# The second channel group's products of a gated dynamic convolution, from stacked 12-bit parts on the whole array to plain float32 on half of its rows

## The chip, the cores and the metric

One core of a Trainium2 chip runs the kernel: TensorE (PE in the profile, its weight loads PEld), VectorE (DVE), ScalarE (ACT), GpSimd (POOL) and SyncE (SP), which here only issues DMAs. The metric is the device time in microseconds from the first to the last instruction of the core. Three runs of the kernel before took 647.55, 649.92 and 651.01 us; the median is 649.92.

## The reference, cut to what matters

Eight sequences of 4224 rows with 192 channels (D), 8 heads of 24 channels. First a dynamic convolution whose weights are a softmax over 7 taps for each row and head, then a gated value path:

```
w   = softmax(weight_gen, axis=-1)                    # (B, S, 8, 7)
x1  = sum over k of w[.., k] * x[row - 6 + k]         # per head, 24 channels
gate = sigmoid(sum over k of conv_w[k] * x1[row - 4 + k])   # 5 taps per channel
val  = x1 @ w_val                                     # 192 x 192
out  = (gate * val) @ w_out                           # 192 x 192
```

All of it is float32 to the reader; weights of the value path come as float64 and are rounded.

## The kernel before, in words

**Tiling.** The rows are cut into blocks of 384 (BLK), and two blocks make a macro; there are 44 macros (NM). Channels live in partitions, in two groups. Group 0 ("A" tiles) is 128 channels of one block, so a macro has two such slices. Group 1 ("B" tiles) is the other 64 channels, those of the macro's first block in partitions 0 to 63 and those of its second block in 64 to 127. Tiles A, B and S (a staging tile for the channels of the last two heads) are allocated for a pair of macros, an even one and the odd one behind it, and rotate through two buffers: the tile of macros 6 and 7 takes the place of that of macros 2 and 3.

**Stages of a macro.** `bank` (L355) does the dynamic convolution as 16 small matmuls for each of four PSUM banks (tile pa, three buffers); `evac` (L393, L395, L399) copies them into A, B and S on ACT, and `moves` sends parts of S into A and B by DMA. `tap0` (ACT, L421, L424) and `tap` (DVE, L429) build the gate's argument in aA and aB, `sigm` (ACT, L433) the gate. `split_a` writes A as a high part of 12 bits (hi, ACT, L440) and the rest (lo, POOL, L441). `split_b` does the same for B through `stack`, which puts the high part of a block's 64 channels in its own half of the partitions and the low part in the other half (tile q, ACT L447, POOL L448), and `gsplit` does it for the gated values of group 1 (tile g, the same two lines).

**Products.** `val` (L462) makes block k's values for group 0 in five fp32r matmuls of 384 columns: two from q, three from hi and lo; for group 1 (k = 2) it uses plain float32 (L464 on the whole array, L466 on two halves of its columns, one per block). `gv` (DVE, L473) multiplies by the gate. `omm` (L489 to L491) makes two chunks of 128 output rows per call: for each one two fp32r matmuls from g (256 columns, against woh and wob) and one float32 matmul from aA (192 columns). There are three calls per macro, each with one PSUM tile po out of two buffers, and `oev` (ACT, L499) copies each into ot, which goes out by DMA.

**What sets the order.** The kernel schedules by hand: `at(t, f)` notes a piece of work with a time in macros, PLAN gives the offsets, and the pieces are emitted in order of time. Every engine then executes its own instructions strictly in the order emitted, and waits where a tile that it reads is not written yet, or where a buffer that it takes over still has a reader.

Of the kernel before, what the change touches and what calls it, by code (L numbers as in the profile page):

```python
# [16 lines left out]
# The order in which the parts of the macros' work are emitted: each at the macro's index plus a number from here.  # L17
# [7 lines left out]
    splitB=2.7981,  # L25
# [5 lines left out]
    gsplit=3.8257,  # L31
# [8 lines left out]
    spo=(2.2858, 3.439),  # L40
# [14 lines left out]
def tile_dynconv_gated_moe(  # L55
# [9 lines left out]
    nc = tc.nc  # L65
# [78 lines left out]
    def order_weights():  # L144
        """Rows of the weights in DRAM in the order of their channels in the partitions."""
# [16 lines left out]
    def convert_weights(raw, cs, v, w):  # L162
        """raw, float64 in pairs of words (low, high), rounded to float32 in columns cs of wf."""
# [19 lines left out]
    def split_weights():  # L183
        """The columns of w_val in the order of the channels in the partitions: towards the first group as sums
        of two parts of 12 bits each, towards the second as they are. The second group's rows of w_out as such
        sums too."""
        units = []

        def runs(dst, src, q0, q1):
            """Quadrants q0 .. q1 - 1 of the columns: (dst, src) for both runs of channels in them."""  # L190
            d = dst.rearrange("p (a c) -> p a c", c=Q)
            return ((d[:, :, 0:C], src[:, C * q0:C * q1].rearrange("p (a c) -> p a c", c=C)),
                    (d[:, :, C:Q], src[:, c6 + HC * q0:c6 + HC * q1].rearrange("p (a c) -> p a c", c=HC)))
# [7 lines left out]
        for g in (1, 0):  # L201
            for (h, v), (l, _) in zip(runs(wvh[:, g], wf[:, g, 0:D], 0, 4), runs(wvl[:, g], wf[:, g, 0:D], 0, 4)):
                units.append(lambda h=h, v=v: nc.scalar.copy(out=h, in_=v))
                units.append(lambda h=h, l=l, v=v: nc.gpsimd.tensor_tensor(
                    out=l, in0=v, in1=h.bitcast(FP32), op=ALU.subtract))
            if g == 1:
                for b in range(2):
                    hs = slice(HD * b, HD * b + HD)
                    units.append(lambda b=b, hs=hs: nc.scalar.copy(out=wvb[b][hs], in_=wvl[hs, 1].bitcast(FP32)))
        s = wf[:, 1, D:2 * D]  # L210
        out_units = [lambda: nc.scalar.copy(out=woh[:, 0:D], in_=s)]
        for b in range(2):
            hs = slice(HD * b, HD * b + HD)
            out_units.append(lambda b=b, hs=hs: nc.gpsimd.tensor_tensor(
                out=wob[b][hs, 0:D], in0=s[hs], in1=woh[hs, 0:D].bitcast(FP32), op=ALU.subtract))
        return units, out_units
# [150 lines left out]
    def pair(i, name, shape):  # L367
        """The tile of that name of macros i and i ^ 1."""
# [12 lines left out]
    def stir(n):  # L381
        """Work of no effect that keeps the clock of the tensor engine up while the first loads are on the way."""
# [18 lines left out]
    def moves(i, g):  # L401
        """Fill the holes of macros i - 1 and i, or of i alone where it is the only one left."""
# [40 lines left out]
    def stack(src, dst, eng):  # L443
        """dst[:, u]: the high part of block u's half of src in its own half, the low part in the other."""
        for u in range(2):
            own, oth = slice(HD * u, HD * u + HD), slice(HD - HD * u, P - HD * u)
            nc.scalar.copy(out=dst[own, u], in_=src[own])  # L447
            eng.tensor_tensor(out=dst[oth, u], in0=src[own], in1=dst[own, u].bitcast(FP32), op=ALU.subtract)  # L448

    def split_b(i):  # L450
        s = st[i]
        s["q"] = work.tile([P, 2, BLK], FP32R, name="q")
# [209 lines left out]
```

## Time and profile before

| What | Value |
|---|---|
| median of three runs | 649.92 us (647.55 to 651.01) |
| the profiled execution's own time, its span | 650.0 us |
| mean granted TensorE clock | 0.971 |
| PE busy | 582.7 us |
| DVE busy | 601.7 us |
| ACT busy | 438.0 us |
| POOL busy | 376.6 us |
| start of the fourth macro's L464, of the 41st's | 106.31 us, 604.28 us |

The profile is one execution. An engine's busy time is the union of its instructions; those of PE overlap, so the sum over its lines is more than its busy time. Each macro has one L464 on PE, so the starts of L464 cut the span into macros: in the text, a macro's period runs from one L464 to the next. Times in a row are microseconds from the start of the span.

### The profile page before, as it was taken

The page shows a single profiled execution, that of the slowest core. Times are in us where ns is not written, and L with a number is a line of the kernel's source. Part 1 is how long each engine was busy: PE and PEld are TensorE (multiplying, and loading weights), DVE is VectorE, ACT ScalarE, POOL GpSimd, SP SyncE. Part 2 cuts the span into 40 slices and gives each one's busy share as a digit, 9 for nine tenths or more (in the row PEclk, how much of TensorE's full clock was granted, in tenths as well). Part 3 has the DMA queues.
Part 4 walks back from the last instruction along what each step waited for, and adds up shares of the span by engine and source line. Part 5 has one row for each costly group of instructions (what it writes and reads, how often), then busy time and mean ns, then how long its engine had stood idle before and what let it go on. Part 6 is the DMA issues. An engine that isn't in the chain of part 4 may idle for free.

```text
span 650.0 us, 18233 instructions
## 1 busy us (share of the span) xinstructions
PE 582.7 (90%) x7422; PEld 459.1 (71%) x7422; DVE 601.7 (93%) x653; ACT 438.0 (67%) x789; POOL 376.6 (58%) x292
## 2 busy tenths in 40 slices
PE   1356699998998999997999979998998999999976
PEld 0345477876787778775778857787876887788766
DVE  7867999999999899998999989998999998898994
ACT  4436396687748687586776768757966676667763
POOL 9154744774755645572665727556656556455673
PEclk9986799999999999999999999999998999999998
DMA  6879967997896968987598876997878658754313
GB/s 191 225 244 176 315 154 167 282 247 155 176 291 197 203 145 206 295 227 154 125 275 214 224 158 129 247 248 188 197 196 288 156 135 196 168 123 114 86 44 110
DMA packets 126914, 124.65 MB, mean 192 GB/s; under 512 B 9390, under 2 KB 121354, under 8 KB 126062
## 3 DMA queue, kind: packets, MB, share of 16 engines
q1 hardware_dynamic: 122970, 101.25, 65.3%
q0 software_dynamic: 3840, 22.23, 9.2%
q8 instruction: 59, 0.97, 0.7%
q14 instruction: 25, 0.20, 0.1%
q10 hardware_dynamic: 20, 0.01, 0.0%
HBM read 67.12 MB, written 50.36 MB: 181 GB/s over the span
## 4 chain that ended last, share of the span: by engine, by line
PE 45%; DVE 22%; DMA 19%; issue 4%; SPq 4%; ACT 4%; POOL 1%; DVEq 0%; ACTq 0%; POOLq 0%
PE pa L355 21%; DVE aA L429 9%; PE po L491 7%; DVE aB L429 6%; PE pv L462 5%; DMA tb<-zd 4%; DMA A<-S 4%; PE po L489 4%; DMA wt<-in_weight_gen_dram 3%; DMA zd<-zt 3%; PE pv L464 3%; PE pv L466 3%; PE po L490 3%; DVE zt L280 2%; SPq L334 2%
## 5 line engine op out<-in xcount | busy, mean ns | idle before, releaser
L355 PE MATMUL pa<-tb,xt 106*32 106x96 f32 (+1 forms) x5632 | 267.9, 357 | 37.4 <-ACT wt L260 22.2
L355 PEld LDWEIGHTS pa<-tb,xt 106*32 106x32 f32 x5632 | 206.7, 129 | 100.3 <-issue 63.1
L429 DVE SCALAR_TENSOR_TENSOR aA<-A,wf,aA 128x768 f32<-128x768 f32 x176 | 226.2, 1286 | 2.5 <-ACT aA L421 2.5
L429 DVE SCALAR_TENSOR_TENSOR aB<-B,wf,aB 128x384 f32<-128x384 f32 x176 | 193.5, 1100 | 0.0
L448 POOL TENSOR_TENSOR q<-B,q 64x384 fp32r<-64x384 f32 x88 | 112.3, 1277 | 99.6 <-ACT q L447 66.1
L441 POOL TENSOR_TENSOR lo<-A,hi 128x768 fp32r<-128x768 f32 x44 | 93.8, 2132 | 101.9 <-issue 35.2
L448 POOL TENSOR_TENSOR g<-aB,g 64x384 fp32r<-64x384 f32 x88 | 126.6, 1439 | 12.9 <-ACT g L447 6.4
L491 PE MATMUL po<-wf,aA 128*128 128x192 f32 x528 | 131.1, 330 | 2.1 <-DVE aA L473 2.1
L489 PE MATMUL po<-woh,g 128*128 128x256 f32 x264 | 98.9, 374 | 17.6 <-ACT ot L499 12.9
L491 PEld LDWEIGHTS po<-wf,aA 128*128 128x128 f32 x528 | 81.8, 191 | 2.6 <-DVE aA L473 2.5
L499 ACT COPY ot<-po 128x384 f32<-128x384 f32 x132 | 62.7, 476 | 25.2 <-PE po L491 24.2
L489 PEld LDWEIGHTS po<-woh,g 128*128 128x128 f32 x264 | 50.4, 191 | 35.4 <-ACT ot L499 15.2
L490 PE MATMUL po<-wob,g 128*128 128x256 f32 x264 | 74.4, 282 | 0.0
L393 ACT COPY A<-pa 128x388 f32<-128x388 f32 x88 | 41.2, 481 | 46.3 <-PE pa L355 27.5
L399 ACT COPY S<-pa 64x388 f32<-64x388 f32 x88 | 42.2, 479 | 29.9 <-PE pa L355 29.3
L473 DVE TENSOR_TENSOR aA<-pv,aA 128x384 f32<-128x384 f32 x88 | 48.1, 547 | 7.3 <-ACT aA L433 6.3
L490 PEld LDWEIGHTS po<-wob,g 128*128 128x128 f32 x264 | 50.6, 192 | 0.0
L421 ACT ACTIVATE aA<-A,wf 128x768 f32<-128x768 f32 x44 | 41.4, 941 | 12.7 <-DMA A<-S 9.1
L447 ACT CAST g<-aB 64x384 fp32r<-64x384 f32 x88 | 45.0, 512 | 4.6 <-DVE aB L473 2.7
L395 ACT COPY B<-pa 128x388 f32<-128x388 f32 x44 | 21.3, 483 | 38.0 <-DVE aB L429 17.8
L433 ACT ACTIVATE aA<-aA 128x768 f32<-128x768 f32 x44 | 37.4, 851 | 13.6 <-DVE aA L429 13.4
L447 ACT CAST q<-B 64x384 fp32r<-64x384 f32 x88 | 44.5, 506 | 1.1
(74 smaller groups left out, 711.0 us busy)
## 6 DMA issues: line engine op xcount, KB each, us to landing
xt<-in_x_dram SPq DMA_DIRECT2D x35, 672.0 KB
out_dram<-ot SPq DMA_DIRECT2D x39, 576.0 KB
tb<-zd SPq DMA_DIRECT2D x240, 88.0 KB
zd<-zt POOLq DMA_DIRECT2D x21, 968.0 KB, 6.8
wt<-in_weight_gen_dram SPq DMA_DIRECT2D x6, 1092.0 KB
A<-S SPq DMA_DIRECT2D x84, 48.5 KB
xt<-in_x_dram SPq DMA_DIRECT2D x5, 588.0 KB
out_dram<-ot SPq DMA_DIRECT2D x8, 288.0 KB
```

What stands on the lines that cost most here:

```text
L355: nc.tensor.matmul(out=pa[Q * c:Q * c + Q, at:at + n], lhsT=xb[0:KR, j, C * h:C * h + Q], rhs=t[0:KR, j, PAD + skip:PAD + skip + n, h], st ...
L399: nc.scalar.copy(out=t[:, 2 * m + u, :], in_=pa[HD * u:HD * u + HD, 0:W])
L421: nc.scalar.activation(out=s["aA"], in_=s["A"][:, :, 0:BLK], func=AF.Copy, scale=cw[:, 0, 0:1])
L429: nc.vector.scalar_tensor_tensor(out=a, in0=src, scalar=cw[:, g, j:j + 1], in1=a, op0=ALU.mult, op1=ALU.add)
L441: nc.gpsimd.tensor_tensor(out=s["lo"], in0=a, in1=s["hi"].bitcast(FP32), op=ALU.subtract)
L447: nc.scalar.copy(out=dst[own, u], in_=src[own])
L448: eng.tensor_tensor(out=dst[oth, u], in0=src[own], in1=dst[own, u].bitcast(FP32), op=ALU.subtract)
L473: nc.vector.tensor_tensor(out=a, in0=s["pv", k][:, 0:BLK], in1=a, op=ALU.mult)
L489: nc.tensor.matmul(out=po[:, v, :], lhsT=s["g"][:, u, cs], rhs=woh, start=True, stop=False)
L490: nc.tensor.matmul(out=po[:, v, :], lhsT=s["g"][:, u, cs], rhs=wob[u], start=False, stop=False)
L491: nc.tensor.matmul(out=po[:, v, 0:D], lhsT=s["aA"][:, u, cs], rhs=woa, start=False, stop=True)
L499: nc.scalar.copy(out=ot[:, k * OPU:(k + 1) * OPU, :], in_=s["po", k][:, :, 0:D])
```

## The change

The parts of group 1 are no longer split. `split_b`, `gsplit` and `stack` are gone with their tiles q and g, and so are the split weights of that group and three memsets of them. `val` now handles both blocks in one call: for each block one float32 matmul on the 64 rows of the array that hold the block's half of B (`tile_position=(64 * k, 0)`), then the three fp32r matmuls from hi and lo as before. `omm` is called twice per macro instead of three times. Each call takes two PSUM tiles, one per block, and makes two chunks of each block (the second call one): float32 matmuls from aA on the whole array, then float32 matmuls from aB on half of the rows for each block, block 0 and block 1 in turn. `oev` copies both tiles. The PLAN's other numbers are the same. Behind all work stands a new function `probe`: 68 matmuls on a zeroed tile pz, whose results nobody reads. The separate sending of the last macro's output in three pieces is gone; it goes as one.

```
@@ PLAN
-    splitB=2.7981,
-    gsplit=3.8257,
-    spo=(2.2858, 3.439),
@@ tiles
-    wvh = const.tile([P, 2, P], FP32R, name="wvh")
-    wvl = const.tile([P, 2, P], FP32R, name="wvl")
-    wvb = [const.tile([P, P], FP32R, name=f"wvb{i}") for i in range(2)]
+    wvh = const.tile([P, P], FP32R, name="wvh")
+    wvl = const.tile([P, P], FP32R, name="wvl")
+    wvb = const.tile([P, P], FP32, name="wvb")
-    WO = 256
-    woh = const.tile([P, WO], FP32R, name="woh")
-    wob = [const.tile([P, WO], FP32R, name=f"wob{i}") for i in range(2)]
+    pz = const.tile([P, 800], FP32, name="pz")
+    wob = wf[:, 1, D:2 * D]
...
-    def val(i, k):
+    def val(i, kinds):
         s = st[i]
-        pv = ps_v.tile([P, 512], FP32, name="pv")
-        if k < 2:
-            ops = [(wvh[:, 1], s["q"][:, k]), (wvb[k], s["q"][:, k]),
-                   (wvh[:, 0], s["hi"][:, k]), (wvh[:, 0], s["lo"][:, k]), (wvl[:, 0], s["hi"][:, k])]
-            for n, (w, r) in enumerate(ops):
-                nc.tensor.matmul(out=pv[:, 0:BLK], lhsT=w, rhs=r, start=(n == 0), stop=(n == len(ops) - 1))
...
+        for k in kinds:
+            hs = slice(HD * k, HD * k + HD)
+            nc.tensor.matmul(out=s["pv", k][:, 0:BLK], lhsT=wvb[hs], rhs=s["B"][hs, HALO:W], start=True, stop=False,
+                             tile_position=(HD * k, 0))
+        for k in kinds:
+            ops = [(wvh, s["hi"][:, k]), (wvh, s["lo"][:, k]), (wvl, s["hi"][:, k])]
+            for n, (w, r) in enumerate(ops):
+                nc.tensor.matmul(out=s["pv", k][:, 0:BLK], lhsT=w, rhs=r, start=False, stop=(n == len(ops) - 1))
...
-    OPU = 2
+    OUNITS = ((0, 1), (2,))
     def omm(i, k):
         s = st[i]
-        po = ps_o.tile([P, OPU, WO], FP32, name="po")
-        for v in range(OPU):
-            u, j = divmod(k * OPU + v, CPB)
-            cs = slice(CH * j, CH * j + CH)
-            nc.tensor.matmul(out=po[:, v, :], lhsT=s["g"][:, u, cs], rhs=woh, start=True, stop=False)
-            nc.tensor.matmul(out=po[:, v, :], lhsT=s["g"][:, u, cs], rhs=wob[u], start=False, stop=False)
-            nc.tensor.matmul(out=po[:, v, 0:D], lhsT=s["aA"][:, u, cs], rhs=woa, start=False, stop=True)
+        po = [ps_o.tile([P, 2, 256], FP32, name="po") for _ in range(2)]
+        for u in range(2):
+            for v, j in enumerate(OUNITS[k]):
+                nc.tensor.matmul(out=po[u][:, v, 0:D], lhsT=s["aA"][:, u, CH * j:CH * j + CH], rhs=woa, start=(v == 0),
+                                 stop=False, skip_group_check=True)
+        for v, j in enumerate(OUNITS[k]):
+            for u in range(2):
+                hs = slice(HD * u, HD * u + HD)
+                nc.tensor.matmul(out=po[u][:, v, 0:D], lhsT=s["aB"][hs, CH * j:CH * j + CH], rhs=wob[hs], start=False,
+                                 stop=True, skip_group_check=True, tile_position=(HD * u, 0))
...
+    def probe():
+        def four(rhs, n):
+            for _ in range(4):
+                pa = ps_a.tile([P, 512], FP32, name="pa")
+                for c in range(4):
+                    nc.tensor.matmul(out=pa[Q * c:Q * c + Q, 0:n], lhsT=pz[0:106, 0:Q], rhs=rhs, start=True, stop=True,
+                                     tile_position=(0, Q * c))
+        z = pz[0:106]
+        four(z[:, 0:96], 96)
+        four(z[:, 0:768].rearrange("p (a b) -> p a b", b=16)[:, :, 0:2], 96)
+        four(z[:, 0:192].rearrange("p (a b) -> p a b", b=2)[:, :, 0], 96)
+        four(z[:, 0:122], 122)
+        for _ in range(4):
+            pv = ps_v.tile([P, 512], FP32, name="pv")
+            nc.tensor.matmul(out=pv[:, 0:D], lhsT=pz.bitcast(FP32R)[:, 0:P], rhs=pz.bitcast(FP32R)[:, 0:D], start=True, stop=True)
...
-        at(sh + i + PLAN["splitB"], split_b, i)
-        for k, tt in zip((2, 0, 1), span(i, "val", 3)):
-            at(sh + tt, val, i, k)
+        tv = span(i, "val", 3)
+        at(sh + tv[0], val, i, (2,))
+        at(sh + tv[1], val, i, (0, 1))
+        for k, tt in zip((2, 0, 1), tv):
             at(sh + tt + PLAN["gvlag"], gv, i, k)
-        at(sh + i + PLAN["gsplit"], gsplit, i)
...
-    for t in (*wvb, woh, *wob):
-        nc.gpsimd.memset(t.bitcast(FP32), 0.0)
+    nc.gpsimd.memset(pz, 0.0)
...
     for _, _, f, a in sorted(ev, key=lambda e: e[:2]):
         f(*a)
+    probe()
```

**ACT, from the copies of an even macro's banks on, before.** Names carry buffer numbers: B_3744 is the tile of a new pair of macros, in the buffer that B_3086 had; pa_3722 is the bank with kind 2; in brackets is what the row waits for (DMAHW are DMAs).

```order
L399 COPY S_3719<-pa_3699 64x388
L395 COPY B_3744<-pa_3722 128x388 [waits DVE_49,PE_49,Pool_49]
L421 ACTIVATE aA_3746<-A_3442,wf_95 128x768 [waits DMAHW4_49,DMAHW5_49,DMAHW3_49,DMAHW2_49]
L433 ACTIVATE aB_3521<-aB_3521 128x384
L440 CAST hi_3770<-A_3442 128x768
L393 COPY A_3774<-pa_3751 128x388 [waits DVE_49,PE_49]
L393 COPY A_3774<-pa_3776 128x388 [waits PE_49]
L499 COPY ot_3813<-po_3795 128x384 [waits PE_49]
L433 ACTIVATE aA_3581<-aA_3581 128x768
```

The same place now. Lines behind `split_weights` have moved up by 14 and more: the copy to B is L381, tap0 of A is L407, the sigmoid L419, hi L426, the copy to A L379, the copies to ot L481.

```order
L385 COPY S_3695<-pa_3677 64x388
L381 COPY B_3720<-pa_3698 128x388 [waits DVE_49,PE_49,Activation_49]
L407 ACTIVATE aA_3722<-A_3455,wf_92 128x768 [waits DMAHW6_49,DMAHW7_49,DMAHW5_49,DMAHW4_49]
L419 ACTIVATE aB_3527<-aB_3527 128x384
L426 CAST hi_3744<-A_3455 128x768 [waits Pool_49]
L379 COPY A_3748<-pa_3725 128x388 [waits DVE_49,Pool_49]
L379 COPY A_3748<-pa_3750 128x388
L481 COPY ot_3792<-po_3769 128x384
L481 COPY ot_3792<-po_3770 128x384
L419 ACTIVATE aA_3578<-aA_3578 128x768
```

ACT's sequence is the same but for the casts of q and g and a second copy to ot. What moved is the PE wait: before, every copy out of PSUM had its own; now the copies from pa_3725, pa_3750, po_3769 and po_3770 have none, because the wait of the copy to B already covers all of them. It waits for the last reader of B_3125 in the buffer that it takes over, which is the second L444 of the next fence.

**PE, the products behind the four banks of the same macro, before** (pv_3806 and pv_3847 are the two blocks' values; these are the rows ahead of and into the second).

```order
L491 MATMUL po_3795<-wf_95,aA_3414 128x192
L462 MATMUL pv_3806<-q_3662,wvh_85 128x384
L462 MATMUL pv_3806<-q_3662,wvb0_87 128x384
L462 MATMUL pv_3806<-hi_3603,wvh_85 128x384
L462 MATMUL pv_3806<-lo_3604,wvh_85 128x384
L462 MATMUL pv_3806<-hi_3603,wvl_86 128x384
L489 MATMUL po_3816<-woh_91,g_3674 128x256
```

And now (L465 and L470 are `omm` on aA and aB, L444 and L449 `val` on B and on hi and lo):

```order
L470 MATMUL po_3770<-wf_92,aB_3378 128x192
L444 MATMUL pv_3781<-B_3125,wvb_87 128x384
L444 MATMUL pv_3782<-B_3125,wvb_87 128x384
L449 MATMUL pv_3781<-hi_3600,wvh_85 128x384
L449 MATMUL pv_3781<-lo_3601,wvh_85 128x384 [waits Pool_49]
L449 MATMUL pv_3781<-hi_3600,wvl_86 128x384
L449 MATMUL pv_3782<-hi_3600,wvh_85 128x384
L449 MATMUL pv_3782<-lo_3601,wvh_85 128x384
L449 MATMUL pv_3782<-hi_3600,wvl_86 128x384
L465 MATMUL po_3808<-wf_92,aA_3427 128x192 [waits PE_49,Activation_49]
```

B is now read by `val` on PE, behind the macro's four banks and the first call of `omm`, where before ACT and POOL had taken their copy q of it earlier. And the second call of `omm` (po_3808) waits for ACT: its two PSUM tiles are those of the first call, which ACT has to copy out first.

More of the change, by code (lines that the diff above doesn't have):

```diff
@@ L200, in split_weights @@
                 units.append(lambda d=d, v=v: nc.scalar.copy(out=d, in_=v))
[L201 to L216, printed above, removed]
+        for d, v in runs(wvb, wf[:, 1, 0:D], 0, 4):
+            units.append(lambda d=d, v=v: nc.scalar.copy(out=d, in_=v))
+        for (h, v), (l, _) in zip(runs(wvh, wf[:, 0, 0:D], 0, 4), runs(wvl, wf[:, 0, 0:D], 0, 4)):
+            units.append(lambda h=h, v=v: nc.scalar.copy(out=h, in_=v))
+            units.append(lambda h=h, l=l, v=v: nc.gpsimd.tensor_tensor(
+                out=l, in0=v, in1=h.bitcast(FP32), op=ALU.subtract))
+        return units
     ROW = H * K
@@ L441, in split_a @@
         nc.gpsimd.tensor_tensor(out=s["lo"], in0=a, in1=s["hi"].bitcast(FP32), op=ALU.subtract)
[L443 to L450, printed above, removed]
-        s = st[i]
-        s["q"] = work.tile([P, 2, BLK], FP32R, name="q")
-        stack(s["B"][:, HALO:W], s["q"], nc.gpsimd)
-    def val(i, k):
-        s = st[i]
-        pv = ps_v.tile([P, 512], FP32, name="pv")
-        if k < 2:
-            ops = [(wvh[:, 1], s["q"][:, k]), (wvb[k], s["q"][:, k]),
-                   (wvh[:, 0], s["hi"][:, k]), (wvh[:, 0], s["lo"][:, k]), (wvl[:, 0], s["hi"][:, k])]
-            for n, (w, r) in enumerate(ops):
-                nc.tensor.matmul(out=pv[:, 0:BLK], lhsT=w, rhs=r, start=(n == 0), stop=(n == len(ops) - 1))
-        else:
+    def val(i, kinds):
+        s = st[i]
+        for k in kinds:
+            s["pv", k] = ps_v.tile([P, 512], FP32, name="pv")
+        if kinds == (2,):
+            pv = s["pv", 2]
             nc.tensor.matmul(out=pv[:, 0:BLK], lhsT=wvd, rhs=s["B"][:, HALO:W], start=True, stop=False)
@@ L467, in val @@
                                  stop=True, tile_position=(0, HD * u))
-        s["pv", k] = pv
+            return
+        for k in kinds:
+            hs = slice(HD * k, HD * k + HD)
+            nc.tensor.matmul(out=s["pv", k][:, 0:BLK], lhsT=wvb[hs], rhs=s["B"][hs, HALO:W], start=True, stop=False,
+                             tile_position=(HD * k, 0))
+        for k in kinds:
+            ops = [(wvh, s["hi"][:, k]), (wvh, s["lo"][:, k]), (wvl, s["hi"][:, k])]
+            for n, (w, r) in enumerate(ops):
+                nc.tensor.matmul(out=s["pv", k][:, 0:BLK], lhsT=w, rhs=r, start=False, stop=(n == len(ops) - 1))
     def gv(i, k):
@@ L498, in oev @@
         ot = s["ot"]
-        nc.scalar.copy(out=ot[:, k * OPU:(k + 1) * OPU, :], in_=s["po", k][:, :, 0:D])
-        if i == NM - 1 and len(parts(i)) == 1:
-            (b, r, _, _), = parts(i)
-            r += k * OPU * CH
-            nc.sync.dma_start(out=out[b, r:r + OPU * CH, :].rearrange("(t p) d -> p t d", p=P),
-                              in_=ot[:, k * OPU:(k + 1) * OPU, :])
-        elif (k + 1) * OPU == 2 * CPB:
+        j, n = OUNITS[k][0], len(OUNITS[k])
+        for u in range(2):
+            nc.scalar.copy(out=ot[:, CPB * u + j:CPB * u + j + n, :], in_=s["po", k][u][:, 0:n, 0:D])
+        if k + 1 == len(OUNITS):
             for b, r, w0, nw in parts(i):
@@ L547, in tile_dynconv_gated_moe @@
             at(sh + i + PLAN["sig" + n], sigm, i, g)
-        at(sh + i + PLAN["splitB"], split_b, i)
         at(sh + i + PLAN["splitA"], split_a, i)
-        for k, tt in zip((2, 0, 1), span(i, "val", 3)):
-            at(sh + tt, val, i, k)
+        tv = span(i, "val", 3)
+        at(sh + tv[0], val, i, (2,))
+        at(sh + tv[1], val, i, (0, 1))
+        for k, tt in zip((2, 0, 1), tv):
             at(sh + tt + PLAN["gvlag"], gv, i, k)
-        at(sh + i + PLAN["gsplit"], gsplit, i)
-        n = 2 * CPB // OPU
-        for k, tt in enumerate(span(i, "out", n)):
+        for k, tt in enumerate(span(i, "out", len(OUNITS))):
             at(sh + tt, omm, i, k)
@@ L628, in tile_dynconv_gated_moe @@
     conv = [convert_weights(raw[:, :, c], c, nc.vector, nc.gpsimd if k < 2 else nc.vector) for k, c in enumerate(cs)]
-    sv, so = split_weights()
-    for key, us in (("cvc", conv[2]), ("cvv", conv[0]), ("cvo", conv[1]), ("spv", sv), ("spo", so)):
+    for key, us in (("cvc", conv[2]), ("cvv", conv[0]), ("cvo", conv[1]), ("spv", split_weights())):
         lo, hi = PLAN[key]
```

4 lines of the change are left out of this document (removed).

## The prediction

> **What bounds the kernel now.** I read the page's busy shares first, then a table of stretches with the periods of single macros, then the chain of waits through one of them, then ACT's sequence in order of time.
>
> ```profile
> 106.31:604.28 497.97, 481.56 (x6221) 379.67 (x6217) 477.07 (x510) 352.49 (x644) 292.96 (x211) 0.99 0.78 198
> 526.81:539.71 12.90, 12.90 (x173) 10.16 (x169) 11.64 (x12) 9.00 (x17) 7.40 (x6) 1.00 0.62 151
> 186.26:201.27 15.01, 13.15 (x173) 10.08 (x169) 15.01 (x17) 8.29 (x17) 9.23 (x8) 1.00 0.90 315
> 375.10:393.42 18.32, 14.29 (x172) 11.25 (x169) 15.70 (x20) 12.32 (x18) 5.41 (x5) 0.91 0.64 140
> 604.28:650.03 45.75, 36.08 (x252) 29.76 (x248) 35.44 (x36) 25.98 (x48) 24.75 (x18) 0.96 0.25 72
> ```
>
> The columns are the stretch, its length, the busy time of PE, PEld, DVE, ACT and POOL, the granted clock, and the DMAs' share and GB/s. The usual macro takes 12.90 us and PE is busy for all of it: PE sets the pace. A macro with softmax work can take 15.01, with DVE busy throughout, and the worst takes 18.32. The middle holds 37 macros (from the fourth L464 to the 41st), so 37 x 12.90 = 477.3 us are PE's, and 20.7 of its 497.97 are not. Inside a macro the chain is:
>
> ```profile
> 565.61 0.84 PE pv L464 x2
> 566.45 0.80 PE pv L466 x4
> 567.25 2.98 PE pa L355 x64
> 570.22 0.31 PE po L489
> 570.53 0.11 PE po L490
> 570.65 0.33 PE po L491 x2
> ...
> 571.53 0.88 PE pv L462 x5
> ...
> 575.53 2.99 PE pa L355 x61
> ```
>
> It is PE alone. The products take 570.22 to 575.53, 5.31 us; L464, L466 and the four banks take the other 7.61.
>
> **PE's own work barely changes.** The row of L491 gives 0.33 us for a float32 matmul of 192 columns, that of L462 0.88/5 = 0.176 for an fp32r one of 384, that of L490 0.11 for one of 256. Removed per macro are six L489 and six L490 at 0.11 and four L462 on q at 0.176: 2.0 us. Added are three pairs on half of the rows in `omm` and one pair of 384 columns in `val`. The trace has no matmul on half of the rows; the nearest row is L466, two matmuls on half of the columns each, which take 0.80 together, no longer than one. I take a pair for the price of one: 3 x 0.33 + 0.65 = 1.64. Each change of the array's layout costs too: L464 takes 0.84 where 384 columns at L491's rate are 0.66, and the first L489 0.31 where L490 takes 0.11, so about 0.2 a change. One such change stands ahead of the products now, and three more come inside them (whole, half, whole, half). The products become 0.20 + 4 x 0.33 (L465) + 0.18 + 0.66 (two pairs, L470) + 0.65 (L444) + 0.18 + 6 x 0.176 (L449) + 2 x 0.33 + 0.18 + 0.33 = 5.4 us, and a macro takes 13.0 instead of 12.9. Bounds: 12.7, if the changes of layout hide behind a full queue; 14.6, if the pairs don't overlap at all (1.64 more, a rival below).
>
> **ACT now stands still in every second macro.** This term decides. The copy into a new pair's tile B waits until all readers of the old tile are done. Its last PE reader was L464, the next thing on PE; now it is L444, behind L464, L466, two banks and the first `omm`: 0.84 + 0.80 + 2.98 + 0.20 + 4 x 0.33 + 0.18 + 0.66 + 0.65 = 7.6 us later. ACT executes in order, so behind this copy wait tap0, the sigmoid, hi, two copies to A and the two copies to ot; and PE's second `omm` waits for those to ot. ACT's rows in order of time say how long that backlog is:
>
> ```profile
> 312.08 0.48 ACT L395 COPY B<-pa 128x388 f32<-128x388 f32 x1
> 312.46 0.95 ACT L421 ACTIVATE aA<-A,wf 128x768 f32<-128x768 f32 x1
> 313.30 0.51 ACT L433 ACTIVATE aB<-aB 128x384 f32<-128x384 f32 x1
> 313.71 0.82 ACT L440 CAST hi<-A 128x768 fp32r<-128x768 f32 x1
> 314.44 0.49 ACT L393 COPY A<-pa 128x388 f32<-128x388 f32 x1
> ```
>
> From start to start: copy to B 0.38, tap0 0.84, sigmoid 0.41, hi 0.73; the two copies to A 0.38 each, and the first copy to ot 0.48 to its end. Together 3.6 us. The hand-overs come on top: at most the 0.18 by which L464's 0.84 exceeds its 0.66, for the last result to drain, and 0.06 from ACT back to PE (in the rows below ACT's copy ends at 387.94 and PE starts at 388.00), 0.25 in all. PE has only a change of layout and six L449 to do meanwhile, 0.18 + 1.06 = 1.2. So it stands for 3.6 + 0.25 - 1.2 = 2.7 us. The tiles that meet this wait are those of macros 6, 8, ... 42 (the earlier ones find a fresh buffer, or their readers stand earlier), 19 waits, all in the middle: 19 x 2.7 = 51 us. Bounds for one: 1.7 (no hand-over, and pieces that overlap more) and 4 (DVE late with what the sigmoid needs).
>
> In two of these macros (that of 375.10 us is one), the softmax's exponential stands between ACT's two copies to A and joins the backlog:
>
> ```profile
> 383.88 1.28 ACT L260 ACT_TABLE_LOAD   x1
> 385.17 2.02 ACT L260 ACTIVATE wt<-wt 128x2184 f32<-128x2184 f32 x1
> 387.10 0.47 ACT L393 COPY A<-pa 128x388 f32<-128x388 f32 x1
> 387.46 0.48 ACT L499 COPY ot<-po 128x384 f32<-128x384 f32 x1
> ```
>
> That is 2 x 3.3 = 6.6 us.
>
> **The clock.** A PE that stood idle can come back slow. Three times in the trace it waited for ACT's copies, for 4.03, 1.84 and 1.85 us, and then did the same six products:
>
> ```profile
> 388.00 0.58 PE L489 MATMUL po<-woh,g 128*128 128x256 f32 x1 [4.03 <-ACT ot L499]
> ...
> 390.43 0.93 PE L355 MATMUL pa<-tb,xt 106*32 106x100 f32 x16
> ...
> 496.32 0.39 PE L489 MATMUL po<-woh,g 128*128 128x256 f32 x1 [1.84 <-ACT ot L499]
> ...
> 498.05 0.57 PE L355 MATMUL pa<-tb,xt 106*32 106x100 f32 x8
> ...
> 196.97 0.39 PE L489 MATMUL po<-woh,g 128*128 128x256 f32 x1 [1.85 <-ACT ot L499]
> ...
> 198.29 0.55 PE L355 MATMUL pa<-tb,xt 106*32 106x100 f32 x8
> ```
>
> They took 2.43, 1.73 and 1.32 us: 1.1 lost, 0.4, nothing. For waits of 2.7 us I charge 0.5 each, 9.5 in all; bounds are nothing and 19 x 1.1 = 21. The Trainium skill, "TensorE: Matmul & The Clock Gate", section "HAM oscillation", warns of idle gaps over some 3.4 us; if only those cost anything, the 2.7 us here are free and the sum is 9.5 us lower. The trace agrees for the gap of 4.03 us, while the one of 1.84 was not free.
>
> **What becomes cheaper.** ACT loses the casts to q and g, POOL all of L448. POOL's work holds up DVE where they meet:
>
> ```profile
> L429 DVE SCALAR_TENSOR_TENSOR aB<-B,wf,aB x176: 519/901/2412, 52.4 to 635.5; 128x384 f32<-128x384 f32 x176
> L429 DVE SCALAR_TENSOR_TENSOR aA<-A,wf,aA x176: 920/1009/2527, 56.9 to 638.5; 128x768 f32<-128x768 f32 x176
> L448 POOL TENSOR_TENSOR q<-B,q 64x384 fp32r<-64x384 f32 x88 | 112.3, 1277 | 99.6 <-ACT q L447 66.1
> L448 POOL TENSOR_TENSOR g<-aB,g 64x384 fp32r<-64x384 f32 x88 | 126.6, 1439 | 12.9 <-ACT g L447 6.4
> ```
>
> The numbers behind x176 are the shortest, the median and the longest duration in ns: a tap on 384 columns takes 519 undisturbed and up to 2412. With POOL's 239 us gone, DVE keeps ahead of PE in softmax macros too, so the 20.7 us of the middle that were not PE's go; a sum of 13.0 us macros has them out already. The copies of two small output tiles in place of one hide in ACT's idle time (352 of 498 us busy). Only the two ends gain openly:
>
> ```profile
> 60.15 0.43 POOL q L448
> 61.23 1.62 POOL q L448
> ...
> 65.62 8.91 DMA zd<-zt
> ...
> 631.70 1.35 POOL q L448
> 633.13 1.19 POOL q L448
> 634.39 1.61 POOL g L448
> ...
> 646.40 0.48 ACT ot L499
> ```
>
> At the start POOL's work on q stands ahead of the DMA at 65.62 on the chain, which goes some 4 us earlier without it: -4, from 0 to -5. In the tail the chain runs through three L448 from 631.70 to 636.00, and DVE ahead of it gets quicker too: -6, from 0 to -10. Against this, PE's probe follows the last `omm`: 16 groups of four small matmuls at 2.98/8 = 0.37 a group (two banks are eight such groups), and four of 192 columns at 0.17, make 6.6 us, where the last `omm` stood 3.6 us ahead of the end (646.40 to 650.03). Not all of that difference is added, since the last output DMA, now in one piece, ends later too: +2.5, from 0 to +4.
>
> **The sum** goes against the profiled execution's 650.0 us, which is also the runs' median (649.92). The middle becomes 37 x 13.0 + 51 + 6.6 + 9.5 = 548 instead of 498: +50. The ends give -4 - 6 + 2.5 = -7.5. That makes 692.
>
> **Rivals.**
> *The wait costs PE nothing, and the kernel is faster.* For it: ACT, DVE and POOL are all relieved. It decides as soon as ACT is through its backlog within PE's 1.2 us, or the second `omm` finds its tiles free. The middle is then 37 x 13.0 = 481, 17 less than before: 650 - 17 - 7.5 = 625. Against it: 3.6 us of ACT's rows, and the waits as they stand in the order of both engines.
> *The wait is mostly absorbed,* at 1 us each and half of the exponential's price: 650 - 17 + 19 + 3 - 7.5 = 648.
> *The halves don't overlap.* 1.64 us more in each of 37 macros: 692 + 61 = 753. For it: no row shows half of the rows. Against it: L466 and L355, whose matmuls on parts of the columns do overlap.
>
> **How the numbers follow.** The forecast has 0.80. Its bounds (waits of 1.7 to 4 us, -19 and +25; macros of 12.7 to 13.3, -11 and +11; clock -9.5 and +11; ends -8 and +9), which will not all fall on one side, give it 665 to 718. Nothing lost has 0.09, mostly absorbed 0.06, halves that don't overlap 0.05. The range from 662 to 718 leaves out these three. Half a per cent (3.2 us) is about what a measurement of this kernel can tell from no change. Slower: 0.80 + 0.05 and half of the absorbed case, 0.88; same 0.03; faster 0.09.
>
> **What would show it.** Periods that alternate between about 13.0 and 16 us; in each second macro ACT idle for 6 to 8 us ahead of the copy to B (now L381), released by PE's L444, and then PE's L465 idle for 2 to 3 us, released by ACT's ot (L481), 19 times. The two L444, and each two L470, starting within some ns of each other. DVE busy near 500 us, POOL near 140. It is wrong if no wait of L381 exceeds 2 us, if the periods are even, or if the two halves of a pair stand one behind the other.

## The result, and the profile after

The changed kernel takes 715.12 us (median; 714.36 to 716.07), the kernel before, beside it, 650.46 (647.55 to 651.11). The ratio is 1.0986, with a 95% interval from 1.0946 to 1.1026: the change makes the kernel 10% slower. The profiled execution took 715.64 us, 713.8 of them within its span. Here and below a median is over all runs of a kernel, and a ratio leaves out a run more than 1.5% longer than the kernel's fastest, of which there is one each in the two runs e5_head and e9_valapart.

The page's busy times of the changed kernel, first:

```profile
PE 607.8 (85%) x7554; PEld 425.4 (60%) x7554; DVE 509.8 (71%) x653; ACT 349.5 (49%) x654; POOL 141.5 (20%) x108
```

Every engine but PE is busy for much less time than before (DVE 601.7, ACT 438.0 and POOL 376.6 us then; DVE with the same 653 instructions). Yet the span grew by 64 us: 25 of them show as busy time of PE, and 39 as PE standing idle. The view of waits says who waited for whom; behind the colon stand the total in us, the number of waits and the longest one:

```profile
DVE aB L454 <- ACT aB L419: 134.2, 23, 8.8
ACT B L381 <- issue: 129.1, 16, 8.1
PE po L465 <- ACT ot L481: 57.4, 22, 5.8
ACT S L385 <- PE pa L341: 43.1, 43, 8.7
ACT B L381 <- PE pv L444: 24.2, 3, 8.1
```

ACT's copy to B waits 19 times (16 + 3) for about 8 us each. Only three times does the view name PE's L444 as the releaser; for the other 16 it says "issue", which means that the view saw nothing to blame. A row of the timeline settles it below. Behind that copy DVE waits for ACT's sigmoid, 5.8 us on average, and PE for ACT's copies to ot; 19 of these 22 waits of PE lie in the middle, 54.1 us of the 57.4.

The table of stretches puts a price on this. The columns are the stretch, its length, the busy time of PE, PEld, DVE, ACT and POOL, the granted clock, and the DMAs' share and GB/s:

```profile
112.04:669.82 557.78, 499.71 (x6220) 348.12 (x6216) 396.94 (x502) 278.37 (x533) 94.39 (x61) 0.95 0.71 176
353.55:369.33 15.78, 13.28 (x172) 8.97 (x168) 9.44 (x12) 6.74 (x14) 3.44 (x3) 1.00 0.67 183
383.06:399.97 16.91, 14.41 (x173) 9.98 (x169) 8.29 (x12) 6.74 (x14) 2.38 (x1) 0.90 0.90 234
399.97:412.96 12.99, 12.99 (x173) 9.16 (x169) 11.09 (x15) 7.04 (x14) 2.56 (x2) 1.00 0.45 106
320.36:340.58 20.22, 14.41 (x172) 10.11 (x169) 12.11 (x16) 11.41 (x17) 2.58 (x2) 0.83 0.48 104
157.93:172.60 14.67, 13.23 (x172) 9.16 (x168) 14.60 (x19) 11.73 (x17) 2.03 (x2) 1.00 0.70 153
70.14:101.03 30.89, 23.95 (x250) 16.42 (x249) 23.31 (x29) 12.90 (x22) 3.88 (x5) 0.78 0.70 192
669.82:713.80 43.98, 39.52 (x384) 27.25 (x380) 28.82 (x39) 18.86 (x39) 5.88 (x3) 1.00 0.26 80
```

The first row is the middle, from the fourth L437 (before: L464) to the 41st: 557.78 us for 37 macros instead of 497.97. The next five are single macros. One with the wait takes 15.8 us (second row) or up to 16.9 (third; the clock shows 0.90 there), one without it 12.99 (fourth), one with wait and exponential 20.22 (fifth), and a macro behind a wait that also has softmax work 14.67, with DVE busy for all but 0.07 of it (sixth). The seventh row is a stretch of the start, from the second macro's L437 to the third's, 30.89 us instead of 22.38. The last row is the tail, 43.98 instead of 45.75.

Through a macro with the wait the chain of waits (start, length, what) reads:

```profile
382.74 8.07 issue
390.81 0.04 ACT B L381
...
391.19 0.94 ACT aA L407
392.13 0.41 ACT aB L419
392.54 0.72 ACT hi L426
393.26 0.77 ACT A L379 x2
394.03 0.39 ACT ot L481
394.42 0.04 issue
394.46 1.65 PE po L465 x4
```

In the timeline of the same macro (start, length, and in brackets the idle time before and its releaser) the "issue" gets a name:

```profile
389.91 0.81 PE L444 MATMUL pv<-B,wvb 64*128 64x384 f32 x4
...
390.65 0.44 PE L449 MATMUL pv<-hi,wvh 128*128 128x384 f32 x1
...
390.81 0.48 ACT L381 COPY B<-pa 128x388 f32<-128x388 f32 x1 [8.08 <-issue]
...
394.46 1.65 PE L465 MATMUL po<-wf,aA 128*128 128x192 f32 x4 [2.50 <-ACT ot L481]
```

The pair of L444 ends at 389.91 + 0.81 = 390.72, the copy to B starts at 390.81. From there the chain runs through ACT's backlog alone to the copy to ot, and PE stands for 2.50 us.

### The profile page after: what moved, and what is told of

It reads as the page before. It is cut to its first block, busy times and chain, and to the rows that moved or that the text cites. A ratio compares the mean times of both kernels' runs of the same rounds, so it can differ in the third digit from the quotient of the medians.

```text
span 713.8 us, 18186 instructions
## 1 busy us (share of the span) xinstructions
PE 607.8 (85%) x7554; PEld 425.4 (60%) x7554; DVE 509.8 (71%) x653; ACT 349.5 (49%) x654; POOL 141.5 (20%) x108
## 4 chain that ended last, share of the span: by engine, by line
PE 46%; issue 18%; DMA 12%; ACT 9%; DVE 8%; SPq 6%; ACTq 0%; POOL 0%; DVEq 0%; POOLq 0%
PE pa L341 21%; PE po L465 9%; PE po L470 5%; PE pv L449 3%; DMA tb<-zd 3%; SPq L320 3%; DMA A<-S 3%; DMA zd<-zt 3%; DVE aA L415 3%; ACT aA L407 2%; PE pv L437 2%; PE pv L444 2%; PE pv L439 2%; SPq L401 2%; ACT A L379 2%
## 5 line engine op out<-in xcount | busy, mean ns | idle before, releaser
L415 DVE SCALAR_TENSOR_TENSOR aA<-A,wf,aA 128x768 f32<-128x768 f32 x176 | 185.6, 1055 | 6.4 <-ACT aA L407 6.4
L465 PE MATMUL po<-wf,aA 128*128 128x192 f32 x528 | 117.4, 358 | 63.3 <-ACT ot L481 57.4
L415 DVE SCALAR_TENSOR_TENSOR aB<-B,wf,aB 128x384 f32<-128x384 f32 x176 | 143.4, 815 | 3.1 <-ACT aB L410 3.0
L465 PEld LDWEIGHTS po<-wf,aA 128*128 128x128 f32 x528 | 88.9, 199 | 89.7 <-ACT ot L481 64.3
L454 DVE TENSOR_TENSOR aB<-pv,aB 128x384 f32<-128x384 f32 x44 | 24.3, 552 | 134.3 <-ACT aB L419 134.2
L481 ACT COPY ot<-po 128x192 f32<-128x192 f32 (+1 forms) x176 | 61.9, 406 | 89.2 <-PE po L470 77.7
L381 ACT COPY B<-pa 128x388 f32<-128x388 f32 x44 | 21.2, 483 | 164.2 <-issue 129.1
L470 PE MATMUL po<-wf,aB 64*128 64x192 f32 x528 | 71.2, 376 | 0.0
L454 DVE TENSOR_TENSOR aA<-pv,aA 128x384 f32<-128x384 f32 x88 | 48.2, 548 | 24.9 <-PE pv L449 17.0
L379 ACT COPY A<-pa 128x388 f32<-128x388 f32 x88 | 40.7, 483 | 35.6 <-PE pa L341 35.2
L470 PEld LDWEIGHTS po<-wf,aB 64*128 64x128 f32 x528 | 43.1, 196 | 21.8 <-issue 21.8
L444 PE MATMUL pv<-B,wvb 64*128 64x384 f32 x176 | 38.4, 495 | 4.6 <-DVE aA L454 4.6
L407 ACT ACTIVATE aA<-A,wf 128x768 f32<-128x768 f32 x44 | 41.3, 939 | 1.8 <-DMA A<-S 1.8
L437 PE MATMUL pv<-B,wvd 128*128 128x384 f32 x88 | 41.9, 559 | 0.0
L439 PE MATMUL pv<-A,wvm 128*64 128x384 f32 x176 | 38.1, 512 | 0.0
L419 ACT ACTIVATE aA<-aA 128x768 f32<-128x768 f32 x44 | 38.1, 865 | 0.1
L266 DVE TENSOR_TENSOR zt<-wt,mx 128x616 f32<-128x616 f32 (+2 forms) x25 | 32.5, 1299 | 6.7 <-DMA zd<-zt 6.6
L426 ACT CAST hi<-A 128x768 fp32r<-128x768 f32 x44 | 36.2, 823 | 0.0
```

Of the source, the lines that this page charges most:

```text
L379: nc.scalar.copy(out=pair(i, "A", [P, 4, W])[:, 2 * m + kind, :], in_=pa[:, 0:W])
L407: nc.scalar.activation(out=s["aA"], in_=s["A"][:, :, 0:BLK], func=AF.Copy, scale=cw[:, 0, 0:1])
L415: nc.vector.scalar_tensor_tensor(out=a, in0=src, scalar=cw[:, g, j:j + 1], in1=a, op0=ALU.mult, op1=ALU.add)
L437: nc.tensor.matmul(out=pv[:, 0:BLK], lhsT=wvd, rhs=s["B"][:, HALO:W], start=True, stop=False)
L439: nc.tensor.matmul(out=pv[HD * u:HD * u + HD, 0:BLK], lhsT=wvm, rhs=s["A"][:, u, HALO:W], start=False, stop=True, tile_position=(0, HD * u))
L444: nc.tensor.matmul(out=s["pv", k][:, 0:BLK], lhsT=wvb[hs], rhs=s["B"][hs, HALO:W], start=True, stop=False, tile_position=(HD * k, 0))
```

## The experiments

The theory: the middle is longer because PE's L444 has become the last reader of tile B, and ACT, in order, stands behind the copy into that tile. The first rival: the longer time is PE's own, from half-row matmuls and the layout changes around them, and the wait is a symptom. A second question came with the profile: why the start, which should have become shorter, is 5.7 us longer.

### A third buffer for B

```
-                pairs[k] = work.tile(shape, FP32, name=name)
+                pairs[k] = work.tile(shape, FP32, name=name, bufs=3 if name == "B" else 2)
```

> The changed kernel with three buffers for tile B instead of two, so that the copy into a new B has no reader to wait for. Theory (the copy to B waits for L444 and holds up ACT's queue, and PE's second omm behind it): no wait of the copy to B over 2 us, macros of about 13.0 us throughout, no 15.8; the 19 waits of 2.8 us, their slow clock (some 10 us) and 2 x 3.3 us of exponentials go, so 715 - 53 - 10 - 7 = 645, between 636 and 653. Rival (the two PSUM tiles per omm couple PE to ACT in any case): macros of 15 us and more remain, 690 or above.

Measured: 643.82 us, ratio 0.989 (0.9855 to 0.9925). Only the buffer count differs from the changed kernel, and 71 us are gone. The middle in the table of stretches:

```profile
115.46:598.79 483.33, 481.39 (x6220) 341.63 (x6216) 397.22 (x505) 282.59 (x533) 94.48 (x61) 1.00 0.81 203
```

And from the view of waits, all that the copy to B waits for:

```profile
ACT B L381 <- PE pa L341: 19.4, 42, 0.7
```

No copy to B waits for L444 any more; PE idles for 2 us of 483, and a macro takes 12.99. This is the theory's number. The rival of PE's own work falls: the half-row matmuls are all still there.

### The same buffer in the kernel before

The same line is changed in the kernel before, nothing else.

> The kernel before with three buffers for tile B. Its copy to B waits 12.7 us in all for L464 and for POOL's q, 17.8 for DVE, none of it in the macros of 12.9 us that PE fills. Theory: within 0.5% of 650, since PE and DVE set its pace. Rival: the waits for the old tile are on the path of the macros over 12.9 us, up to 10 us faster.

Measured: 650.35 us, ratio 1.0015 (0.9989 to 1.004). The third buffer is worth nothing by itself. It pays only where L444 holds the tile.

### The copy to B later, with two buffers

```
-            at(t[k] + PLAN["evlag"], evac, i, kind)
+            at(t[k] + PLAN["evlag"] + (0.3351 if kind == 2 and i % 2 == 0 and i >= 6 else 0), evac, i, kind)
```

In the even macros from number 6 on, the copy to B is emitted 0.34 macros later: behind ACT's two copies to A, ahead of its copies to ot.

> The changed kernel with two buffers for B as it is, but the copy to B of macros 6, 8, ... 42 emitted behind ACT's two copies to A, ahead of the copies to ot. The wait for L444 stays; what stands behind it on ACT is only the copy to B (0.38) and the first copy to ot (0.48). Theory (the cost is what queues behind the waiting copy): 0.38 + 0.48 + 0.25 of hand-over against PE's 1.2, so PE waits next to nothing, macros near 13.0 to 13.3, 645 to 655 in all. Rival (the lateness of the tile itself costs, whatever stands behind it): 700 or above.

Measured: 646.44 us, ratio 0.9935 (0.9906 to 0.9965). The copy still waits for L444, as the view of waits shows:

```profile
ACT B L381 <- PE pv L444: 40.3, 17, 2.5
```

These are 17 waits of up to 2.5 us, now under the name of L444, yet the middle takes 489.64 us: 6 more than with the third buffer, instead of 74 more. Of these 6, 3.9 stand in one macro with the exponential, which takes 18.89 us here and 14.97 there. So it is not the lateness of the tile that costs, but what is queued behind the copy on ACT: with tap0, the sigmoid, hi and the two copies to A ahead of it, the same dependence costs next to nothing in the other macros.

### Each half of the change alone

One kernel has only the output on half rows (the kernel before, with the changed kernel's `omm` and `oev`, and without g). The other has only val on half rows (the changed kernel with the earlier `omm`, `oev` and g, without the probe). Both have two buffers for B.

> The kernel before with only the output's second group on half rows (val still with stacked parts through q; two buffers for B). Theory (the loss belongs to val's half alone, since L444 is the new last reader of B): no wait of the copy to B, macros of 12.9 to 13.1 us, POOL and ACT relieved of g: 640 us (634 to 652). Rival (the output's half brings loss of its own, by two po tiles that must both be free and two copies to ot instead of one): 665 us or more.

> The changed kernel with only val's second group on half rows (the output still with stacked parts through g, no probe; two buffers for B). Theory (the wait of the copy to B for L444 is val's): every second macro is stretched by 2 to 4 us, since ACT's backlog behind the wait now holds the copies to g too: 715 us (695 to 740). Rival (the wait costs only together with the output's two po tiles): 650 us (640 to 660).

Measured: output alone 649.16 us, ratio 0.9973 (0.9937 to 1.0009); val alone 698.98 us, ratio 1.0724 (1.0677 to 1.077). A usual macro of the output alone, in the table of stretches:

```profile
177.95:191.17 13.22, 13.22 (x173) 9.38 (x169) 10.66 (x13) 8.04 (x16) 5.81 (x5) 1.00 0.58 166
```

A macro with the wait and one without it, of val alone:

```profile
378.43:393.32 14.89, 13.48 (x172) 9.49 (x169) 9.43 (x11) 7.56 (x15) 5.18 (x3) 1.00 0.81 206
393.32:406.55 13.23, 13.23 (x173) 9.72 (x169) 13.16 (x15) 8.09 (x15) 5.19 (x4) 1.00 0.69 161
```

And from the view of its waits:

```profile
ACT B L390 <- PE pv L460: 138.8, 19, 9.2
PE po L486 <- ACT ot L496: 33.4, 19, 4.7
```

The wait belongs to val's half (L390 and L460 are this kernel's copy to B and its half-row val pair): 19 of them again. With the output alone the copy to B never waits for PE for more than 1.3 us, no longer than in the kernel before. But 699 missed the expected 715 and is just inside its range: PE stands 33.4/19 = 1.76 us per wait instead of 57.4/22 = 2.6, although ACT has the copies to g on top. I had expected the longer backlog to count. Smaller output calls (three per macro, one PSUM tile each) leave PE more to do before it needs ACT's copies, which fits, but no run isolates that. The output alone brought nothing measurable where I expected 10 us less: its macro takes 13.21 us, 0.3 more than before.

### Do the two halves run side by side?

In the first kernel (three buffers for B) the val matmuls of block 0 and block 1 are emitted at two places in every macro. In the second (three buffers, val apart in macros 0 to 2 only, as in the run below) block 0's half-row matmuls of the output stand ahead of block 1's full-row ones:

```
         for u in range(2):
             for v, j in enumerate(OUNITS[k]):
                 nc.tensor.matmul(out=po[u][:, v, 0:D], lhsT=s["aA"][:, u, CH * j:CH * j + CH], rhs=woa, ...)
-        for v, j in enumerate(OUNITS[k]):
-            for u in range(2):
+            for v, j in enumerate(OUNITS[k]):
                 hs = slice(HD * u, HD * u + HD)
                 nc.tensor.matmul(out=po[u][:, v, 0:D], lhsT=s["aB"][hs, ...], rhs=wob[hs], ..., tile_position=(HD * u, 0))
```

> The changed kernel with three buffers for B and the val matmuls of the two blocks emitted at two places in every macro (in the run e5_head: in macros 0 to 2 only), so that no two L444 of different array halves stand next to each other. Theory (a pair of half-row matmuls runs side by side, so one alone lasts as long as the pair, 0.65 us): 0.65 us more for each of some 43 macros, middle macros of 13.6 to 13.7 us instead of 12.99, +28 us beside e5_head: 664 us (659 to 670). Rival (the pair runs one after the other at half the price each): no change beside e5_head, 636 us (632 to 643).

> The kernel of e5_head with the output's half-row matmuls of the first block placed ahead of the second block's full-row matmuls, so that none of the three L470 pairs of a macro stands together. Theory (side by side): each of the three pairs costs its 0.33 us twice, 1.0 us more a macro, middle macros of 13.9 to 14.0 us, +43 us: 679 us (672 to 686). Rival (one after the other at half the price): no change beside e5_head, 636 us (632 to 643).

> The kernel of e9_valapart again, for a profile of its usual time: 664 us and middle macros near 13.65 us if one half-row matmul alone costs its 0.65 us and nothing else; 13.8 us if the two further changes between full rows and half rows cost 0.08 us each as well.

Measured: val apart 664.37 us, ratio 1.0205 (1.0163 to 1.0246); one more execution, with its profile, took 670.3, 6 more than was expected, 4.2 of them in one macro with the exponential (17.97 us); output apart 706.44 us, ratio 1.0871 (1.0843 to 1.0899), above the 672 to 686 that were expected. Beside them stands 636.5 for the kernel in which the pairs stand together (below). PE's timeline of that one more execution with val apart:

```profile
409.29 0.92 PE L470 MATMUL po<-wf,aB 64*128 64x192 f32 x8
410.04 0.80 PE L444 MATMUL pv<-B,wvb 64*128 64x384 f32 x2
410.78 0.44 PE L449 MATMUL pv<-hi,wvh 128*128 128x384 f32 x1
```

Beside it pairs that stand together, from the changed kernel's chain:

```profile
164.89 0.92 PE po L465 x4
165.81 0.85 PE po L470 x8
166.66 0.65 PE pv L444 x4
167.30 1.24 PE pv L449 x6
```

A float32 matmul stands as two instructions, so x2 is one half and x4 a pair. From its start to the start of L449 one half alone takes 410.78 - 410.04 = 0.74 us, and a pair takes the same (390.65 - 389.91 in the changed kernel's timeline above; 0.65 plus the change of layout): the rival "one after the other" is out. The macro with val apart takes 13.81 us instead of 12.99, so 0.82 and not 0.65: in size the second of the two possibilities written down for this execution. In the records the second half of val stands right behind L470, so only one change between half and full rows is added, and not two; the other 0.17 us is its price if it carries all of it. The output's pairs apart cost more than expected in the same way. Their macros take 14.76 us, 1.77 more, and PE is busy for all of it. Three halves alone at 0.33 make 1.0; the other 0.77 comes with four more changes between full and half rows per macro, 0.19 each if they carry all of it.

### The start: val's two blocks apart in macros 0 to 2

In the changed kernel's start PE waits twice at L444 (its timeline; in brackets the idle time before and its releaser):

```profile
73.93 1.65 PE L444 MATMUL pv<-B,wvb 64*128 64x384 f32 x2 [2.19 <-DVE aA L454]
78.02 1.65 PE L444 MATMUL pv<-B,wvb 64*128 64x384 f32 x2 [2.44 <-DVE aA L454]
```

ACT's copies to S are late behind it, as its timeline shows:

```profile
83.51 0.96 ACT L385 COPY S<-pa 64x388 f32<-64x388 f32 x2 [8.67 <-PE pa L341]
```

The two L444 are of block 0 and block 1, each for its own pv tile, and each tile must first be freed by DVE's L454. Before the change, val of block 0 and of block 1 were two pieces of work with a bank between them. Undone for the first three macros, on top of the third buffer for B:

```
-        at(sh + tv[1], val, i, (0, 1))
+        if i < 3:
+            at(sh + tv[1], val, i, (0,))
+            at(sh + tv[2], val, i, (1,))
+        else:
+            at(sh + tv[1], val, i, (0, 1))
```

> The changed kernel with three buffers for B, and in macros 0 to 2 the val matmuls of block 0 and block 1 emitted at two places, as in the kernel before, instead of together. Theory (the later start comes from the joined call: both blocks' first matmuls stand together and PE waits at each for a pv tile that L454 on DVE has not yet freed, with ACT's copies to S behind it): the stretch from the second to the third macro shrinks from 31.5 us towards the 22.4 of the kernel before, by 4 to 9 us, so 637 us (633 to 640). Rival (the later start comes from ACT's exponential and copies to ot, or from the loads, and the waits at pv only show it): 644 us (642 to 646).

Measured: 636.47 us (634.39 without the slowest of four runs), ratio 0.975 (0.9693 to 0.9807), 7.4 us less than with the third buffer alone. The middle and the stretch of the start:

```profile
105.53:587.33 481.80, 481.61 (x6220) 341.42 (x6216) 396.04 (x503) 282.48 (x533) 94.22 (x61) 1.00 0.81 204
69.56:93.47 23.91, 20.83 (x248) 14.38 (x248) 21.19 (x28) 12.79 (x22) 2.64 (x2) 0.93 0.80 229
```

The stretch shrinks from 31.5 to 23.9 us, PE stands idle for 0.2 us of the middle, and the fourth macro starts at 105.5 us. This profile is of the fastest of the four runs. With both halves of the change it starts between 111.3 and 115.5 us in the four kernels whose early val calls are joined, and between 105.5 and 109.3 in the five that keep them apart (val alone, joined, has 110.0). So the joined call is what made most of the start late.

The same edit alone, in the changed kernel with its two buffers:

> The changed kernel (two buffers for B, with probe) with one edit: in macros 0 to 2 the val matmuls of the two blocks at two places, as in the kernel before. Theory (the loss at the start and the wait of the copy to B in the middle are two causes that add): 7 us less than the changed kernel, 708 us (704 to 711), middle still near 558 us. Rival (with two buffers the start is set by the waits of the copies to B, and the two places bring nothing): 715 us (713 to 718).

Measured: 713.37 us, ratio 1.0964 (1.0918 to 1.101). That is only 1.75 less than the changed kernel, inside the rival's range and above the theory's, so the two causes do not simply add. Yet the two places do bring something. The stretch shrinks by 5.2 us (25.74), but with two buffers ACT's copy to B stands in the way here too:

```profile
83.51 0.48 ACT L381 COPY B<-pa 128x388 f32<-128x388 f32 x1 [3.01 <-PE pv L444]
```

PE then waits 2.85 us for ACT's ot at 89.91. The fourth macro starts 3.6 us earlier; of that, 2.5 reach the end of the span.

### The probe

`probe()` is left out: once in the changed kernel, once in the kernel of the 636.47 us.

> The changed kernel without the probe's 68 matmuls at the end (their results are read by nobody). Theory: PE's 6.6 us of probe reach past the last output's DMA by 2.5 us, so 712.5, between 711 and 715. Rival one: the probe hides wholly behind the last output, no change. Rival two: all of it is added, 708.5.

> The kernel of the run beside it (three buffers for B, early val blocks apart) without the probe matmuls. Theory (the probe hides in the time in which the first or last loads and stores are on the way): the same within 1 us as with it. Rival (now that PE bounds the whole program, its 3.8 us count in full): 4 us less than with it, 633 us.

Measured: 716.68 us, ratio 1.1021 (1.0975 to 1.1067), beside 715.12 with the probe; and 636.96 us, ratio 0.9781 (0.9725 to 0.9838), beside 636.47. So it was rival one in the changed kernel, and the theory in the other. The probe costs nothing that these runs can tell (those of the faster kernel spread over 7 to 10 us), since it runs beside the last output DMA. In the changed kernel's tail:

```profile
708.41 3.13 PE L495 MATMUL pa<-pz 106*32 106x96 f32 x128
...
709.08 0.37 SPq L485 DMA_DIRECT2D out_dram<-ot  x1
...
711.47 0.77 PE L504 MATMUL pv<-pz 128*128 128x192 f32 x4
```

The DMA is issued at 709.08 and the span ends at 713.8; PE has finished the probe at 712.24.

## Why the prediction was right, and where it was not

The forecast was 692 us (662 to 718), with "ACT now stands still in every second macro" as the deciding term. The time is 715.1. The mechanism was the one forecast; two terms of the sum were not, both on the same side, and the range held them with 3 us to spare. Point by point:

**"PE's own work barely changes."** Right: 12.99 us for a macro without a wait, 13.0 forecast. The pair at the price of one is right too: the pair of L444 takes the 0.65 us forecast, the two pairs of L470 0.85 with their change of layout (0.84 forecast), the six L449 1.24 with theirs (1.24 forecast).

**"ACT stands still in every second macro."** Right in place, count and size. There are 19 waits of the copy to B, 8.1 us each at most. The backlog behind it is as forecast: the chain goes from 390.81 to 394.42, 3.6 us. A macro with the wait takes 15.81, 2.82 more than one without: PE idles for 2.50, and 0.3 more show as busy time around the stop. Forecast were 2.7. All 19 make 53.6 us against 51.

**The exponential** in two macros: 20.22 - 15.81 - 1.1 for the clock = 3.3 each, as forecast.

**"The clock."** Close in its sum, partly by luck, since the prediction had an average of three waits and no rule. (The trace before has a fourth wait of this kind, of 4.08 us up to 305.56, behind which 0.7 us were lost.) After the 17 idle times of 2.50 us and the two of 5.81, PE's next 16 instructions take 1.78 us nine times, and 2.26 to 2.89 ten times: 9.3 us lost, 9.5 forecast. The same four instructions, after the same idle time, in the timeline of an earlier macro:

```profile
184.01 0.97 PE L465 MATMUL po<-wf,aA 128*128 128x192 f32 x4 [2.50 <-ACT ot L481]
```

Here 0.97, in the row at 394.46 above 1.65. The granted clock (the number behind POOL's) tells the two apart:

```profile
179.45:182.87 3.42, 2.06 (x14) 1.20 (x10) 0.75 (x2) 2.51 (x5) 0.00 (x0) 1.00 1.15 169
182.87:186.28 3.41, 2.27 (x28) 1.65 (x32) 3.38 (x4) 2.95 (x8) 2.39 (x1) 1.00 0.11 22
391.08:394.49 3.41, 0.91 (x7) 0.60 (x5) 1.91 (x3) 3.41 (x8) 1.15 (x1) 1.00 1.10 304
394.49:397.91 3.42, 3.42 (x32) 2.52 (x36) 3.42 (x4) 1.87 (x5) 1.24 (x1) 0.50 1.08 281
```

In this profile the clock is granted in full or by half, and it changes only at times that lie whole multiples of 3.41 us apart; the four rows are windows between such times. The idle time that ends at 394.46 lies within one window, in which PE is busy for 0.91 us, and the next window gets half the clock. The one that ends at 184.01 is cut into 1.36 and 1.14 us by the edge of two windows, and the clock stays. It is so throughout: from the fourth macro on, PE idled for 1.61 us or more in each of the 13 full-clock windows that a slow one follows, and for 1.45 at most in the 139 others. So it is the place of an idle time of 2.50 us among these windows that decides. The same holds for the prediction's two waits of 1.84 and 1.85 us: the first lies within one window, the second is cut into 1.67 and 0.18. In three macros the slow window begins so late that it misses the 16 instructions and meets the banks, which lose nothing by it (2.99 us from 124.87 on, wholly at half clock, 2.98 at full).

The Trainium skill's rule on gaps over some 3.4 us ("TensorE: Matmul & The Clock Gate", "HAM oscillation") would have made this term nothing. The trace does not agree: eight of the 17 idle times of 2.50 us were followed by slow matmuls.

**"DVE keeps ahead of PE in softmax macros too."** This step failed. It mostly holds where ACT does not stand still: with the third buffer and the early val calls apart, macros with softmax work take 12.99 to 13.4 us, and DVE is busy for 12.9 of them at most. (In the profile of the same kernel without the probe, an execution of 641.59 us, three such macros took 14.1, 14.9 and 16.8; PE waited there for DVE, for a DMA and for ACT behind the exponential.) In the changed kernel DVE stands behind ACT's sigmoid for 5.8 us in a macro with the wait, and in the next one it has its own work to make up: the 14.67 us above with DVE at 14.60. The 18 macros between the waits are together 7.75 us longer than 18 x 12.99. About 6 us of this arise at PE's first L465; in the middle the view of waits names DVE's L454 for the five longest:

```profile
PE po L465 <- DVE aA L454: 4.0, 5, 1.4
```

The chain of that macro of 14.67 us runs through it, up to the row at 164.89 shown above:

```profile
163.76 0.61 DVE aB L415
164.37 0.48 DVE aA L454
```

The other 1.8 us are not DVE's: in five of the 18 the half clock of the stop before still lies on the first L437. The prediction followed the wait to PE through ACT's copies to ot and left out the second engine that waits for ACT, which pays one macro later.

With these the middle is accounted for, the last term with both its causes: 37 x 12.99 + 53.6 + 6.6 + 9.3 + 7.75 = 557.9, measured 557.78, forecast 548.

**"What becomes cheaper."** DVE is busy for 509.8 us and POOL for 141.5, near the 500 and 140 forecast.

**The ends**, forecast at -7.5, came out at +4.0, the larger miss. That lies outside the bounds of -8 and +9 given for them. "-4" at the start is the step that failed most: the start is 5.7 us longer. Two things were wrong in it. POOL's DMA to zd moved by only 1.3 us (64.31 instead of 65.62), since with q gone it waits for something else, 4.30 us for the DMAs that still read zd. And the joined val call, to which the sum gave no price, stalls PE where the pv tiles are not free yet; pulled apart, it gave back 5.2 us of that stretch with two buffers and 7.6 with three. In the tail "-6" and "+2.5" were both too large: 43.98 us instead of 45.75, -1.8 in all. The probe hides (it takes 3.8 us, not the 6.6 of the sum), and the tail without POOL's three L448 is only some 2 us shorter (43.7 without the probe).

Middle and ends missed by 9.8 and 11.5 us; with 1.8 us of the execution outside the span that makes 715 out of 692.

**The rivals.** "The wait costs PE nothing" did not come, but its 625 was the better guess of what the change is worth without the wait: 636.5 with a third buffer and the early val calls apart, both engines relieved as that rival said. "The halves don't overlap" is refuted by the two runs that pull the pairs apart.

## What to carry to other kernels

When an operation changes engine, precision or place, ask which instruction is now the last reader of each tile that it reads, and what stands in order behind the instruction that waits for that tile. Here one matmul moved from early to late in the macro cost some 70 us through ACT's queue, and a third buffer took 71 us back, a later place for one copy 69. Follow such a wait to every engine that waits for the blocked one: the one that is not critical in the blocked macro can be the bound in the next. And when two calls are joined, check that their output tiles are free at the same time, above all at the start, where the steady rhythm isn't reached yet.

## What was not expected of the hardware

Pairs of half-row matmuls start 6 to 8 ns apart in the records and cost as much as one (0.74 us either way, with the change of layout). What costs beside them seems to be changing between full-row and half-row matmuls. By the prediction's prices the output alone should make a macro of 12.57 us, val alone 12.85 and both together 12.52; they make 13.21, 13.23 and 12.99. The rest falls on four, two and three such changes, 0.16 to 0.19 us each, as in the two kernels with halves apart (0.17 and 0.19). This is an estimate: no run has such a change by itself, and a weight load that is no longer hidden would look the same.

The same idle time of 2.50 us left PE at full speed nine times and slow eight times, with up to 1.1 us lost, by its place among the windows of 3.41 us in which the clock is granted. In all profiles of this case together, from the fourth macro on, 59 full-clock windows are followed by a slow one, and in each PE had idled for 1.56 us or more; in some 2000 others it had idled for 1.67 at most. So an idle time costs more than itself when about half of one window falls to it.

The probe's 16 groups of four small matmuls take 3.06 us, 0.19 a group, where the banks' groups take 0.37. They read other data (zeros) in partly other layouts, so this case doesn't tell which of the two it is.
